# Sliding-window attention beside a gated MLP on one core: query-key products chunk by chunk in two passes, attention sums in pairs, values reloaded in chunks

## The chip, the cores and the metric

One core of a Trainium2 chip. The metric is the time of one execution in device microseconds (us). A kernel is run several times; quoted times are medians of those runs. Runs are marked fast or slow by their granted TensorE clock and time, and only fast runs are compared.

Names of engines: PE is TensorE's matmul, PEld its weight load, DVE is VectorE, ACT is ScalarE, POOL is GpSimd, SP the engine whose queue issues the DMA transfers.

## The reference

Everything is bf16, S = 2048 rows, D = 640, 32 heads of 20, F = 1536.

```python
xn  = layernorm(x)
q, k, v = split(xn @ wqkv)                       # 32 heads of 20
# each row attends to 8 rows: itself and those 2, 4, ... 14 before it
logits = einsum("bhsd,bhswd->bhsw", q, k_gathered) * 20**-0.5    # masked at the start
attn   = softmax(logits)
o      = einsum("bhsw,bhswd->bhsd", attn, v_gathered)
out = x + o @ wo + ((xn @ w_gate) * (xn @ w_up)) @ w_down
```

## The kernel before

The kernel writes its program in one order; a small scheduler gives each instruction to its engine's list in that order and adds semaphore waits where data demand them. So **each engine, and the SP queue, gets its work in exactly the order written**, and an instruction that waits holds those behind it (seen below on DVE at 154.47 us and on SP's queue at 150.47 us).

- Features lie on partitions, rows along the free dimension, in chunks of 128 features (NCH = 5) and pieces of 512 rows (NJ = 4). DVE multiplies Q by K shifted by an offset w (eight offsets, five chunks: 40 products of 128x2048, tile PRD); PE sums within heads with a 0/1 matrix G of 32 columns, four row pieces side by side in the array (tile LOG).
- Values go through memory (v_scratch) and come back as VX, with offsets laid over partitions. DVE multiplies VX by the attention weights ATX (tile P, 20 units of 128x4096: four row pieces j times five chunks c); PE sums each with a 32-column matrix SEL into OT.
- Between these, PE works on a list of "fill": V projections, gate and up products (`glu`), and output rows (`tail`), which add the down projection and OT times WO, 17 matmuls of 320 columns for half the output width. A tail of row piece j may only start once the five units of piece j are done.

```python
    def qk_logits(w, c, s):                       # one product: 4 matmuls of 32 columns
        lb = 6 + w % 2
        for j in range(NJ):
            ... # PS[32j:32j+32, lb] += G[:, c].T @ PRD[:, s, 512 rows of piece j]
        if c == NCH - 1:
            ... # ACT: LOG[slot_of(w)] = PS[lb] * SCALE; POOL: mask

    def vx_load(j):                               # all 20 values of row piece j, 2600 KB
        dst = VX[:, j % 2]
        ...

    def glu(which, m, j):                         # gate or up: 5 matmuls of 512 columns
        ... # ACT: GSX or USX = PS; DVE later: HT = USX * GSX (at most one held back)

    def tail(t, nb):                              # one half of 128 output rows
        b = bank()
        flush_h()
        ... # 12 matmuls with HT, WD and 5 with OT, WO into PS[b]
        op("dve", lambda e: e.tensor_tensor(o, PS[:, b, 0:DHALF], xr, ALU.add), ...)   # FOUT = PS + XR
        if nb == 1:
            stores.append(dma(...))               # the store, and the load of XR for rows t + 3
    ...
    for i in range(10):                           # the last Q and K projections, all of them first
        proj(i % 2, i // 2, 3)
    ...
    add_gu(0)
    add_gu(1)
    fill.append((0.0, lambda: [xr_load(t) for t in range(NXR)]))    # the first three XR loads
    add_dn(0)
    add_gu(2)
    add_dn(1)
    ...
    order = [(w, c) for w in range(W) for c in range(NCH)]          # offset by offset
    for i, (w, c) in enumerate(order):
        ...
        if c in (1, 4):                           # batches of 2 and 3 products
            for a in ready:
                qk_logits(*a)
            ready = []
        run_fill(1.05)
    for st in softmax_steps():                    # whole width, exp in two halves of the offsets
        st()
        run_fill(1.05)
    for j in range(2):
        vx_load(j)
    for j in range(NJ):
        attn_move(j)
    run_fill(12.0)
    units = [(j, c) for j in range(NJ) for c in range(NCH)]
    pv_mul(*units[0])
    for i, (j, c) in enumerate(units):            # one product, one sum
        run_fill(2.1)
        if i + 1 < len(units):
            pv_mul(*units[i + 1])
        if c == NCH - 1 and j + 2 < NJ:
            vx_load(j + 2)
        pv_sum(j, c)
        units_done[0] += 1
```

Of the kernel before, what the change touches and what calls it, by code (L numbers as in the profile page):

```python
# [195 lines left out]
def build_kernel(nc, A_x, A_wqkv, A_wo, B_x, B_w_gate, B_w_up, B_w_down, out):  # L196
# [28 lines left out]
    VX = sb("VX", [128, 2, DH, VW], at=a_qk)  # L225
# [6 lines left out]
    NP = 2  # L232
    P = sb("P", [128, NP, 4, 2, JB], at=a_pr)
    ATX = sb("ATX", [128, 2, S], at=a_pr + NP * 8 * JB * 2)
# [13 lines left out]
    NGX = 3  # L248
    GSX = sb("GSX", [128, NGX, JB])
    USX = sb("USX", [128, NGX, JB])  # L250
# [40 lines left out]
    def wqkv_load(g):  # L291
        dma(WQKV[:, g], wqkv_src[:, :, g * D:(g + 1) * D], w=[WQKV[:, g]], name=f"ld_wqkv{g}")
# [3 lines left out]
    wqkv_load(0)  # L296
# [74 lines left out]
    bank_ctr = [0]  # L371

    def bank():
        bank_ctr[0] += 1
        return (bank_ctr[0] - 1) % 6
# [55 lines left out]
    def qk_logits(w, c, s):  # L431
        lb = 6 + w % 2
        for j in range(NJ):
            o, x = PS[32 * j:32 * j + 32, lb, :], PRD[:, s, j * JB:(j + 1) * JB]
            op("pe", (lambda o, x, j: lambda e: e.matmul(o, G[:, c, :], x, start=(c == 0), stop=(c == NCH - 1),  # L435
                                                      tile_position=(0, 32 * j)))(o, x, j),
               r=[G[:, c, :], x], w=[o], name=f"lg{w}_{c}_{j}")
        if c == NCH - 1:
            o = LOG[:, slot_of(w), :]
            op("act", lambda e: e.activation(o, PS[:, lb, :], ACT.Copy, scale=SCALE), r=[PS[:, lb, :]], w=[o],  # L440
               name=f"lgev{w}")
            if w > 0:
                m = LOG[0:32, slot_of(w), 0:DIL * w]
                op("pool", lambda e: e.memset(m, NEG), w=[m], name=f"mask{w}")

    def softmax_steps():
# [3 lines left out]
        def bc(t, n):  # L450
            return t.unsqueeze(1).to_broadcast([128, n, JB])

        steps = [
            tt(MX[:], LOG[:, 0:4, :], LOG[:, 4:8, :], ALU.max, "smax1"),
            tt(MY[:], MX[:, 0:2, :], MX[:, 2:4, :], ALU.max, "smax2"),
            tt(MZ[:], MY[:, 0, :], MY[:, 1, :], ALU.max, "smax3"),
        ]
        for h in range(2):
            L = LOG[:, 4 * h:4 * h + 4, :]
            steps.append((lambda L: lambda: op("dve", lambda e: e.tensor_tensor(L, L, bc(MZ[:], 4), ALU.subtract),  # L460
                                            r=[L, MZ[:]], w=[L], name="lsub"))(L))
            steps.append((lambda L: lambda: op("act", lambda e: e.activation(L, L, ACT.Exp), r=[L], w=[L],  # L462
                                            name="exp"))(L))

        def recip(e):
            with nc.allow_low_precision("bf16 softmax reciprocal"):
                return e.reciprocal(RS[:], SM[:, 3, :])  # L467

        steps += [
            tt(SM[:], LOG[:, 0:4, :], LOG[:, 4:8, :], ALU.add, "ssum1"),  # L470
            tt(SM[:, 0:2, :], SM[:, 0:2, :], SM[:, 2:4, :], ALU.add, "ssum2"),
            tt(SM[:, 3, :], SM[:, 0, :], SM[:, 1, :], ALU.add, "ssum3"),
            lambda: op("dve", recip, r=[SM[:, 3, :]], w=[RS[:]], name="rs"),
        ]
        steps.append(lambda: op("dve", lambda e: e.tensor_tensor(LOG[:], LOG[:], bc(RS[:], 8), ALU.mult),
                                r=[LOG[:], RS[:]], w=[LOG[:]], name="attn"))
        return steps

# [36 lines left out]
    def flush_h(keep=0):  # L515
        while len(h_pending) > keep:
            h_pending.pop(0)()
# [227 lines left out]
```

## Time and profile before

| | before |
|---|---|
| time, median of the first 3 runs | 293.34 us (292.68 to 293.87) |
| span of the profiled run | 292.2 us |
| PE busy | 279.0 us, 95% |
| start of the 512-column projections | 49.05 us |
| from there to the last output addition | 240.40 us |

The page gives busy time (first line of each engine) and the span in 40 slices, one digit for the busy tenths of each. PEclk is the granted clock in tenths.

```profile
PE 279.0 (95%) x1968; PEld 155.3 (53%) x1986; DVE 172.2 (59%) x252; ACT 118.3 (40%) x211; POOL 2.3 (1%) x17
...
PE   6899999999999999999949999999999999999996
...
PEclk9799999999999999999989999999999999999999
```

PE is the engine to watch: it is busy for 95% of the span, and most of the other work runs beside it. The digit 4 in the middle of its row, near 150 us, is the one big hole. PE's timeline there (start, duration, engine, line, operation, output and inputs, shapes, count, and in brackets the idle time before it and who ended it):

```profile
144.73 1.24 PE L525 MATMUL PS<-XNT,WU 128*128 128x512 bf16 x5
145.91 0.61 PE L505 MATMUL PS<-P,SEL 128*32 128x512 bf16 x8
147.32 0.62 PE L505 MATMUL PS<-P,SEL 128*32 128x512 bf16 x8 [0.80 <-DVE P L496]
149.52 0.61 PE L505 MATMUL PS<-P,SEL 128*32 128x512 bf16 x8 [1.58 <-DVE P L496]
151.72 1.04 PE L505 MATMUL PS<-P,SEL 128*32 128x512 bf16 x8 [1.59 <-DVE P L496]
152.70 2.84 PE L552 MATMUL PS<-WD,HT 128*128 128x320 bf16 x12
155.37 0.84 PE L552 MATMUL PS<-WO,OT 128*128 128x320 bf16 x5
156.14 0.62 PE L505 MATMUL PS<-P,SEL 128*32 128x512 bf16 x8
```

The fill that needs no attention is used up at 145.9 us; PE has only sums to do and waits for each product. Then its clock is low: the same sum takes 1.04 instead of 0.61 us, the next twelve matmuls 2.84 instead of 1.79.

Two small tools are needed. First, *pace*: in undisturbed stretches 50 full-width matmuls of 512 columns take 10.79 us, 0.2158 each, and 272 of 320 columns 36.96 us, 0.1359 each. All matmuls from 49.05 us on (630 of the first kind, 544 of the second, 80 groups of four narrow ones at 0.2158) come to 227.1 us. Second, *the cost of going narrow and back*: a batch of 8 narrow matmuls takes 0.547 us from its start to that of the next group, 0.115 more than two groups at that pace; and a full-width group after it is 0.11 longer (17 output matmuls 2.42 against 2.31 us). That is 0.225 us per batch, and there are 36. So 227.1 + 36 x 0.225 = 235.2, and of the 240.4 us that PE took, 5.2 are loss.

Where DVE was late, and what PE waited for, is in the view of waits (who waited for whom, total us, times, longest):

```profile
DVE PRD L428 <- ACT KT L386: 7.6, 5, 3.9
DVE SM L448 <- ACT LOG L462: 4.1, 1, 4.1
DVE PRD L428 <- PE PS L435: 4.1, 5, 1.1
PE PS L505 <- DVE P L496: 4.0, 3, 1.6
...
PE PS L393 <- DMA WQKV<-in_A_wqkv_dram: 2.0, 1, 2.0
```

### The profile page before, as it was taken

What the parts mean: (1) busy time and instruction counts of PE and PEld (TensorE: products, weight loads), DVE (VectorE), ACT (ScalarE), POOL (GpSimd) and SP (SyncE); (2) the same over time, 40 slices, a digit from 0 to 9 for tenths busy, and PEclk for the clock granted to TensorE, in tenths of its full rate; (3) what the DMA queues carried; (4) which work ended last, traced back from release to release, by engine and by line L of the source; (5) the groups of instructions that cost most, each with busy time, mean ns of one, the idle gap of its engine ahead of it and who ended that gap; (6) DMA issues with size and microseconds to landing.
All of it is one profiled execution on the core that took longest, in us unless ns stands there. A gap on an engine that the chain in (4) does not pass through costs nothing.

```text
span 292.2 us, 4669 instructions
## 1 busy us (share of the span) xinstructions
PE 279.0 (95%) x1968; PEld 155.3 (53%) x1986; DVE 172.2 (59%) x252; ACT 118.3 (40%) x211; POOL 2.3 (1%) x17
## 2 busy tenths in 40 slices
PE   6899999999999999999949999999999999999996
PEld 2789987433333334444315554334577444577774
DVE  4677793588889994497996999961222121222221
ACT  2255555575455455864531124665300455300000
POOL 2000000000000000000000000000000000000000
PEclk9799999999999999999989999999999999999999
DMA  7715999008998008931329385000012100012211
GB/s 227 246 47 76 372 388 273 5 0 342 369 403 325 1 2 273 358 100 36 100 83 342 110 277 179 2 0 0 2 65 69 47 0 0 2 45 90 70 45 45
DMA packets 29556, 39.57 MB, mean 135 GB/s; under 512 B 4192, under 2 KB 25696, under 8 KB 29536
## 3 DMA queue, kind: packets, MB, share of 16 engines
q1 hardware_dynamic: 29536, 39.29, 40.1%
q8 instruction: 15, 0.25, 0.3%
q14 instruction: 5, 0.04, 0.0%
HBM read 25.07 MB, written 13.16 MB: 131 GB/s over the span
## 4 chain that ended last, share of the span: by engine, by line
PE 82%; DVE 8%; ACT 4%; DMA 2%; issue 2%; SPq 0%; DVEq 0%; ACTq 0%
PE PS L525 27%; PE PS L552 26%; PE PS L381 11%; PE PS L400 7%; PE PS L393 4%; DVE P L496 3%; PE PS L435 3%; PE PS L505 3%; DMA XST<-in_A_x_dram 2%; PE PS L357 2%; DVE SM L448 1%; ACT LOG L462 1%; DVE RS L467 1%; ACT USX L527 1%; ACT GSX L527 1%
## 5 line engine op out<-in xcount | busy, mean ns | idle before, releaser
L525 PE MATMUL PS<-XNT,WU 128*128 128x512 bf16 x237 | 59.5, 379 | 0.2
L525 PE MATMUL PS<-XNT,WG 128*128 128x512 bf16 x230 | 57.7, 379 | 1.1 <-issue 0.6
L552 PE MATMUL PS<-WD,HT 128*128 128x320 bf16 x384 | 58.5, 303 | 0.0
L428 DVE TENSOR_TENSOR PRD<-QT,KT 128x2048 bf16<-128x2048 bf16 x40 | 47.0, 1221 | 11.9 <-ACT KT L386 7.6
L527 ACT ACTIVATE GSX<-PS 128x512 bf16<-128x512 f32 x48 | 28.8, 600 | 45.9 <-PE PS L525 32.3
L552 PEld LDWEIGHTS PS<-WD,HT 128*128 128x128 bf16 x384 | 37.3, 99 | 18.7 <-issue 3.8
L496 DVE TENSOR_TENSOR P<-VX,ATX 128x4096 bf16<-128x4096 bf16 x20 | 45.3, 2284 | 0.0
L556 DVE TENSOR_TENSOR FOUT<-PS,XR 128x320 bf16<-128x320 f32 x32 | 15.7, 492 | 46.4 <-PE PS L552 46.4
L532 DVE TENSOR_TENSOR HT<-USX,GSX 128x512 bf16<-128x512 bf16 x48 | 20.1, 423 | 38.7 <-ACT USX L527 38.7
L525 PEld LDWEIGHTS PS<-XNT,WG 128*128 128x128 bf16 x240 | 22.4, 98 | 30.6 <-issue 4.7
L525 PEld LDWEIGHTS PS<-XNT,WU 128*128 128x128 bf16 x240 | 23.1, 98 | 29.1 <-issue 1.7
L527 ACT ACTIVATE USX<-PS 128x512 bf16<-128x512 f32 x48 | 28.8, 601 | 20.5 <-PE PS L525 20.3
L381 PE MATMUL PS<-XNT,WQKV 128*128 128x512 bf16 x145 | 33.3, 380 | 0.4 <-ACT VST L386 0.2
L552 PE MATMUL PS<-WO,OT 128*128 128x320 bf16 x160 | 27.0, 299 | 0.0
L381 PEld LDWEIGHTS PS<-XNT,WQKV 128*128 128x128 bf16 x150 | 14.0, 98 | 19.0 <-issue 2.1
L400 PE MATMUL PS<-XNT,WQKV 128*128 128x256 bf16 x200 | 23.6, 273 | 0.0
L509 ACT ACTIVATE OT<-PS 128x512 bf16<-128x512 f32 x20 | 11.9, 597 | 24.4 <-PE PS L505 24.4
L400 PEld LDWEIGHTS PS<-XNT,WQKV 128*128 128x128 bf16 x200 | 19.1, 98 | 2.0
L552 PEld LDWEIGHTS PS<-WO,OT 128*128 128x128 bf16 x160 | 15.7, 98 | 6.1
L505 PE MATMUL PS<-P,SEL 128*32 128x512 bf16 x160 | 12.7, 396 | 4.0 <-DVE P L496 4.0
L386 ACT ACTIVATE VST<-PS 128x512 bf16<-128x512 f32 x20 | 11.9, 596 | 11.2 <-PE PS L381 11.2
L393 PE MATMUL PS<-XNT,WQKV 128*128 128x128 bf16 x200 | 13.3, 228 | 2.7 <-DMA WQKV<-in_A_wqkv_dram 2.0
(46 smaller groups left out, 142.6 us busy)
## 6 DMA issues: line engine op xcount, KB each, us to landing
VX<-v_scratch SPq DMA_DIRECT2D x4, 2600.0 KB, 11.1
v_scratch<-VST SPq DMA_DIRECT2D x20, 512.0 KB, 5.1
XST<-in_A_x_dram SPq DMA_DIRECT2D x16, 160.0 KB, 3.8
XR<-in_A_x_dram SPq DMA_DIRECT2D x16, 160.0 KB, 2.5
out_dram<-FOUT SPq DMA_DIRECT2D x16, 160.0 KB, 1.8
WQKV<-in_A_wqkv_dram SPq DMA_DIRECT2D x3, 800.0 KB, 6.6
WG<-in_B_w_gate_dram SPq DMA_DIRECT2D x1, 1920.0 KB, 11.6
WU<-in_B_w_up_dram SPq DMA_DIRECT2D x1, 1920.0 KB, 16.0
```

The lines of the kernel that those rows point to most:

```text
L381: op("pe", (lambda l, x, c: lambda e: e.matmul(PS[:, b, :], l, x, start=(c == 0), stop=(c == NCH - 1)))(l, x, c), r=[l, x], w=[PS[:, b, :] ...
L386: op("act", lambda e: e.activation(o, PS[:, b, :], ACT.Copy), r=[PS[:, b, :]], w=[o], name=f"pev{which}_{m}_{j}")
L393: op("pe", (lambda o, l, x, c: lambda e: e.matmul(o, l, x, start=(c == 0), stop=(c == NCH - 1)))(o, l, x, c), r=[l, x], w=[o], name=f"pp{w ...
L400: op("pe", (lambda l, x, c: lambda e: e.matmul(o, l, x, start=(c == 0), stop=(c == NCH - 1)))(l, x, c), r=[l, x], w=[o], name=f"pw{which}_ ...
L428: op("dve", lambda e: e.tensor_tensor(PRD[:, s, :], QT[:, c, :], k, ALU.mult), r=[QT[:, c, :], k], w=[PRD[:, s, :]], name=f"prod{w}_{c}")
L496: op("dve", lambda e: e.tensor_tensor(P[:, u], vw, a, ALU.mult), r=[v, ATX[:, :, j * JB:(j + 1) * JB]], w=[P[:, u]], name=f"pv{j}_{c}")
L505: op("pe", (lambda o, dq, r: lambda e: e.matmul(o, SEL[:], P[:, u, dq, r, :], start=(r == 0), stop=(r == 1), tile_position=(0, 32 * dq)))( ...
L525: op("pe", (lambda l, x, c: lambda e: e.matmul(PS[:, b, :], l, x, start=(c == 0), stop=(c == NCH - 1)))(l, x, c), r=[l, x], w=[PS[:, b, :] ...
L527: op("act", lambda e: e.activation(X[:, k, :], PS[:, b, :], ACT.Copy), r=[PS[:, b, :]], w=[X[:, k, :]], name=f"guev{which}_{m}_{j}")
L532: h_pending.append(lambda: op("dve", lambda e: e.tensor_tensor(o, USX[:, k, :], GSX[:, k, :], ALU.mult), r=[USX[:, k, :], GSX[:, k, :]], w ...
L552: op("pe", (lambda l, x, i: lambda e: e.matmul(PS[:, b, 0:DHALF], l, x, start=(i == 0), stop=(i == n - 1)))(l, x, i), r=[l, x], w=[PS[:, b ...
L556: op("dve", lambda e: e.tensor_tensor(o, PS[:, b, 0:DHALF], xr, ALU.add), r=[PS[:, b, :], xr], w=[o], name=f"fin{t}_{nb}")
```

## The change

The intent: bring DVE's attention work forward so that PE never runs out of fill, with fewer and longer narrow batches.

- Products go chunk by chunk, four offsets at a time, in two passes; they start as soon as the last projection of a chunk is done. Logits are summed in batches of four products (16 matmuls), in four banks.
- Softmax runs in two halves of the rows, so that the exponentials of one overlap DVE's work on the other. Gate multiplies are held back meanwhile (`h_keep`), in place in HT.
- Values are reloaded in 20 pieces of 520 KB, eight ahead; the load for unit u+8 is issued after the product of unit u. Sums are done in pairs, with three product buffers.
- PE's order is now made by a plan: two counters (`t_pe`, `t_dve`) that add up estimated costs.
- At the start the first weight load is split, and the second tile's normalization goes ahead of the third's statistics.

```diff
-    VX = sb("VX", [128, 2, DH, VW], at=a_qk)
+    NVX = 8
+    VX = sb("VX", [128, NVX, 4, VW], at=a_qk)
 ...
-    wqkv_load(0)
+    wqkv_load(0, 0, 2 * 128)
+    wqkv_load(0, 2 * 128, D)
 ...
+    def vx_load(u):
+        j, c = divmod(u, NCH)
+        dst = VX[:, u % NVX]
 ...
+    def pv_mul(u):
 ...
+        op("dve", lambda e: e.tensor_tensor(p[:], vw, a, ALU.mult), r=[v, at], w=[p[:]], name=f"pv{u}")
+        if u + NVX < NU:
+            vx_load(u + NVX)
 ...
+    ln_apply(1)
     ln_stats_a(2)
-    ln_apply(1)
 ...
-    order = [(w, c) for w in range(W) for c in range(NCH)]
+    order = [(w, c) for h in range(2) for c in range(NCH) for w in range(4 * h, 4 * h + 4)]
 ...
+    for u in range(NVX):
+        vx_load(u)
+    bank_ring[:] = bank_ring + [4, 5]
+    h_keep[0] = NUS - 1
+    for cost, st in softmax_steps():
         st()
-        run_fill(1.05)
+        t_dve[0] += cost
+        run_fill(t_dve[0])
+    h_keep[0] = 1
     for j in range(NJ):
         attn_move(j)
 ...
+    t_dve[0] += 3.0
+    for u in range(0, NU, 2):
+        pv_mul(u)
+        if u:
+            run_fill(t_ready)
+            pv_sum((u - 2, u - 1))
+            t_pe[0] = max(t_pe[0], t_ready) + 1.13
+            units_done[0] += 2
+        pv_mul(u + 1)
+        t_dve[0] += 4.57
+        t_ready = t_dve[0] + 0.2
```

The fill list itself is as before.

More of the change, by code (lines that the diff above doesn't have):

```diff
@@ L231, in build_kernel @@
     PRD = sb("PRD", [128, NPW, S])
-    NP = 2
-    P = sb("P", [128, NP, 4, 2, JB], at=a_pr)
-    ATX = sb("ATX", [128, 2, S], at=a_pr + NP * 8 * JB * 2)
+    PB = [sb("PA", [128, 4, 2, JB], at=a_pr), sb("PB", [128, 4, 2, JB], at=a_pr + 8 * JB * 2),
+          sb("PC", [128, 4, 2, JB], at=a_qk + NVX * 4 * VW * 2)]
+    NP = len(PB)
+    ATX = sb("ATX", [128, 2, S], at=a_pr + 2 * 8 * JB * 2)
     MX = sb("MX", [128, 4, JB], at=a_pr)
@@ L247, in build_kernel @@
     FOUT = sb("FOUT", [128, 2, D])
-    NGX = 3
-    GSX = sb("GSX", [128, NGX, JB])
-    USX = sb("USX", [128, NGX, JB])
+    NUS = 6
+    USX = sb("USX", [128, NUS, JB])
     STATS = sb("STATS", [128, 2, 16], FP32)
@@ L289, in build_kernel, with wqkv_load @@
     wqkv_src = A_wqkv.rearrange("(c p) n -> p c n", p=128)
-    def wqkv_load(g):
-        dma(WQKV[:, g], wqkv_src[:, :, g * D:(g + 1) * D], w=[WQKV[:, g]], name=f"ld_wqkv{g}")
+    def wqkv_load(g, lo=0, hi=D):
+        dst = WQKV[:, g, :, lo:hi]
+        dma(dst, wqkv_src[:, :, g * D + lo:g * D + hi], w=[dst], name=f"ld_wqkv{g}_{lo}")
     x_load(0)
     x_load(1)
-    wqkv_load(0)
+    wqkv_load(0, 0, 2 * 128)
+    wqkv_load(0, 2 * 128, D)
     x_load(2)
@@ L368, in warm @@
                r=[ZERO[:]], w=[PS[:, 5, :]], name="warm")
-    bank_ctr = [0]
+    bank_ring = list(range(6))
     def bank():
-        bank_ctr[0] += 1
-        return (bank_ctr[0] - 1) % 6
+        b = bank_ring.pop(0)
+        bank_ring.append(b)
+        return b
     def proj(which, m, j):
@@ L429, in qk_prod, with qk_logits @@
            r=[QT[:, c, :], k], w=[PRD[:, s, :]], name=f"prod{w}_{c}")
-    def qk_logits(w, c, s):
-        lb = 6 + w % 2
-        for j in range(NJ):
-            o, x = PS[32 * j:32 * j + 32, lb, :], PRD[:, s, j * JB:(j + 1) * JB]
-            op("pe", (lambda o, x, j: lambda e: e.matmul(o, G[:, c, :], x, start=(c == 0), stop=(c == NCH - 1),
-                                                      tile_position=(0, 32 * j)))(o, x, j),
-               r=[G[:, c, :], x], w=[o], name=f"lg{w}_{c}_{j}")
-        if c == NCH - 1:
-            o = LOG[:, slot_of(w), :]
-            op("act", lambda e: e.activation(o, PS[:, lb, :], ACT.Copy, scale=SCALE), r=[PS[:, lb, :]], w=[o],
-               name=f"lgev{w}")
-            if w > 0:
-                m = LOG[0:32, slot_of(w), 0:DIL * w]
-                op("pool", lambda e: e.memset(m, NEG), w=[m], name=f"mask{w}")
+    def qk_logits(batch):
+        for w, c, s in batch:
+            lb = 4 + w % 4
+            for j in range(NJ):
+                o, x = PS[32 * j:32 * j + 32, lb, :], PRD[:, s, j * JB:(j + 1) * JB]
+                op("pe", (lambda o, x, j, c: lambda e: e.matmul(o, G[:, c, :], x, start=(c == 0), stop=(c == NCH - 1),
+                                                             tile_position=(0, 32 * j)))(o, x, j, c),
+                   r=[G[:, c, :], x], w=[o], name=f"lg{w}_{c}_{j}")
+        for w, c, s in batch:
+            if c == NCH - 1:
+                lb = 4 + w % 4
+                o = LOG[:, slot_of(w), :]
+                op("act", (lambda o, lb: lambda e: e.activation(o, PS[:, lb, :], ACT.Copy, scale=SCALE))(o, lb),
+                   r=[PS[:, lb, :]], w=[o], name=f"lgev{w}")
+                if w > 0:
+                    m = LOG[0:32, slot_of(w), 0:DIL * w]
+                    op("pool", (lambda m: lambda e: e.memset(m, NEG))(m), w=[m], name=f"mask{w}")
     def softmax_steps():
@@ L448, in tt @@
             return lambda: op("dve", lambda e: e.tensor_tensor(o, a, b, f), r=[a, b], w=[o], name=name)
-        def bc(t, n):
-            return t.unsqueeze(1).to_broadcast([128, n, JB])
-        steps = [
-            tt(MX[:], LOG[:, 0:4, :], LOG[:, 4:8, :], ALU.max, "smax1"),
-            tt(MY[:], MX[:, 0:2, :], MX[:, 2:4, :], ALU.max, "smax2"),
-            tt(MZ[:], MY[:, 0, :], MY[:, 1, :], ALU.max, "smax3"),
-        ]
-        for h in range(2):
-            L = LOG[:, 4 * h:4 * h + 4, :]
-            steps.append((lambda L: lambda: op("dve", lambda e: e.tensor_tensor(L, L, bc(MZ[:], 4), ALU.subtract),
-                                            r=[L, MZ[:]], w=[L], name="lsub"))(L))
-            steps.append((lambda L: lambda: op("act", lambda e: e.activation(L, L, ACT.Exp), r=[L], w=[L],
-                                            name="exp"))(L))
@@ L465, in recip @@
-        def recip(e):
-            with nc.allow_low_precision("bf16 softmax reciprocal"):
-                return e.reciprocal(RS[:], SM[:, 3, :])
-        steps += [
-            tt(SM[:], LOG[:, 0:4, :], LOG[:, 4:8, :], ALU.add, "ssum1"),
-            tt(SM[:, 0:2, :], SM[:, 0:2, :], SM[:, 2:4, :], ALU.add, "ssum2"),
-            tt(SM[:, 3, :], SM[:, 0, :], SM[:, 1, :], ALU.add, "ssum3"),
-            lambda: op("dve", recip, r=[SM[:, 3, :]], w=[RS[:]], name="rs"),
-        ]
-        steps.append(lambda: op("dve", lambda e: e.tensor_tensor(LOG[:], LOG[:], bc(RS[:], 8), ALU.mult),
-                                r=[LOG[:], RS[:]], w=[LOG[:]], name="attn"))
@@ L477, in softmax_steps, with half, bc, recip @@
-        return steps
+        def half(x):
+            cs = slice(x * JB // 2, (x + 1) * JB // 2)
+            def bc(t, n):
+                return t.unsqueeze(1).to_broadcast([128, n, JB // 2])
+            L, M1, M2, M3 = LOG[:, :, cs], MX[:, :, cs], MY[:, :, cs], MZ[:, cs]
+            S1, S2, R = SM[:, 0:4, cs], SM[:, 0:2, cs], RS[:, cs]
+            def recip(e):
+                with nc.allow_low_precision("bf16 softmax reciprocal"):
+                    return e.reciprocal(R, SM[:, 3, cs])
+            head = [
+                (0.67, tt(M1, L[:, 0:4], L[:, 4:8], ALU.max, "smax1")),
+                (0.4, tt(M2, M1[:, 0:2], M1[:, 2:4], ALU.max, "smax2")),
+                (0.25, tt(M3, M2[:, 0], M2[:, 1], ALU.max, "smax3")),
+                (1.22, lambda: op("dve", lambda e: e.tensor_tensor(L, L, bc(M3, 8), ALU.subtract), r=[L, M3], w=[L],
+                                  name="lsub")),
+                (0.0, lambda: op("act", lambda e: e.activation(L, L, ACT.Exp), r=[L], w=[L], name="exp")),
+            ]
+            rest = [
+                (1.2, tt(S1, L[:, 0:4], L[:, 4:8], ALU.add, "ssum1")),
+                (0.67, tt(S2, S1[:, 0:2], S1[:, 2:4], ALU.add, "ssum2")),
+                (0.4, tt(SM[:, 3, cs], S2[:, 0], S2[:, 1], ALU.add, "ssum3")),
+                (1.75, lambda: op("dve", recip, r=[SM[:, 3, cs]], w=[R], name="rs")),
+                (1.22, lambda: op("dve", lambda e: e.tensor_tensor(L, L, bc(R, 8), ALU.mult), r=[L, R], w=[L],
+                                  name="attn")),
+            ]
+            return head, rest
@@ L479, in attn_move @@
+        (h0, r0), (h1, r1) = half(0), half(1)
+        return h0 + h1 + r0 + r1
     def attn_move(j):
@@ L483, in attn_move @@
             dma(dst, src, r=[src], w=[dst], name=f"atx{j}_{wq}")
-    def vx_load(j):
-        dst = VX[:, j % 2]
-        src = vscr.rearrange("q (h d) s -> (q h) d s", d=DH)[:, :, j * JB:j * JB + VW]
-        dma(dst, src, r=[("vscr", m, q) for m in range(NCH + 1) for q in range(4)], w=[dst], name=f"vx{j}")
-    def pv_mul(j, c):
-        u = (j * NCH + c) % NP
-        v = VX[:, j % 2, 4 * c:4 * c + 4, :]
-        vw = bass.AP(v.tensor, v.offset, [v.ap[0], [VW, 4], [8, 2], [1, JB]])
-        a = ATX[:, :, j * JB:(j + 1) * JB].unsqueeze(1).to_broadcast([128, 4, 2, JB])
-        op("dve", lambda e: e.tensor_tensor(P[:, u], vw, a, ALU.mult),
-           r=[v, ATX[:, :, j * JB:(j + 1) * JB]], w=[P[:, u]], name=f"pv{j}_{c}")
@@ L499, in pv_sum @@
-    def pv_sum(j, c):
-        u = (j * NCH + c) % NP
-        b = 6 + (j * NCH + c) % 2
-        for r in range(2):
-            for dq in range(4):
-                o = PS[32 * dq:32 * dq + 32, b, :]
-                op("pe", (lambda o, dq, r: lambda e: e.matmul(o, SEL[:], P[:, u, dq, r, :], start=(r == 0), stop=(r == 1),
-                                                           tile_position=(0, 32 * dq)))(o, dq, r),
-                   r=[SEL[:], P[:, u, dq, r, :]], w=[o], name=f"I{j}_{c}_{dq}_{r}")
-        o = OT[:, c, j * JB:(j + 1) * JB]
-        op("act", lambda e: e.activation(o, PS[:, b, :], ACT.Copy), r=[PS[:, b, :]], w=[o], name=f"oev{j}_{c}")
+    def vx_load(u):
+        j, c = divmod(u, NCH)
+        dst = VX[:, u % NVX]
+        src = vscr.rearrange("q (h d) s -> (q h) d s", d=DH)[:, 4 * c:4 * c + 4, j * JB:j * JB + VW]
+        dma(dst, src, r=[("vscr", m, q) for m in range(NCH + 1) for q in range(4)], w=[dst], name=f"vx{u}")
@@ new lines, in pv_mul, with pv_sum @@
+    def pv_mul(u):
+        j = u // NCH
+        v, p = VX[:, u % NVX], PB[u % NP]
+        vw = bass.AP(v.tensor, v.offset, [v.ap[0], [VW, 4], [8, 2], [1, JB]])
+        at = ATX[:, :, j * JB:(j + 1) * JB]
+        a = at.unsqueeze(1).to_broadcast([128, 4, 2, JB])
+        op("dve", lambda e: e.tensor_tensor(p[:], vw, a, ALU.mult), r=[v, at], w=[p[:]], name=f"pv{u}")
+        if u + NVX < NU:
+            vx_load(u + NVX)
+    def pv_sum(us):
+        for u in us:
+            b, p = 6 + u % 2, PB[u % NP]
+            for r in range(2):
+                for dq in range(4):
+                    o = PS[32 * dq:32 * dq + 32, b, :]
+                    op("pe", (lambda o, p, dq, r: lambda e: e.matmul(o, SEL[:], p[:, dq, r, :], start=(r == 0), stop=(r == 1),
+                                                                  tile_position=(0, 32 * dq)))(o, p, dq, r),
+                       r=[SEL[:], p[:, dq, r, :]], w=[o], name=f"I{u}_{dq}_{r}")
+        for u in us:
+            j, c = divmod(u, NCH)
+            b = 6 + u % 2
+            o = OT[:, c, j * JB:(j + 1) * JB]
+            op("act", (lambda o, b: lambda e: e.activation(o, PS[:, b, :], ACT.Copy))(o, b), r=[PS[:, b, :]], w=[o],
+               name=f"oev{u}")
@@ L512, in build_kernel, with flush_h @@
     pair_ctr = [0]
     h_pending = []
-    def flush_h(keep=0):
+    h_keep = [1]
+    def flush_h(keep):
+        n = 0
         while len(h_pending) > keep:
             h_pending.pop(0)()
+            n += 1
+        return n
     def glu(which, m, j):
-        k = pair_ctr[0] % NGX
-        T, X = ((WG, GSX), (WU, USX))[which]
+        k = pair_ctr[0] % NUS
+        T = (WG, WU)[which]
+        h = HT[:, j % 2, m, :]
+        o = (h, USX[:, k, :])[which]
         b = bank()
@@ L526, in glu @@
                r=[l, x], w=[PS[:, b, :]], name=f"gu{which}_{m}_{j}_{c}")
-        op("act", lambda e: e.activation(X[:, k, :], PS[:, b, :], ACT.Copy), r=[PS[:, b, :]], w=[X[:, k, :]],
-           name=f"guev{which}_{m}_{j}")
+        op("act", lambda e: e.activation(o, PS[:, b, :], ACT.Copy), r=[PS[:, b, :]], w=[o], name=f"guev{which}_{m}_{j}")
         if which == 1:
             pair_ctr[0] += 1
-            o = HT[:, j % 2, m, :]
-            h_pending.append(lambda: op("dve", lambda e: e.tensor_tensor(o, USX[:, k, :], GSX[:, k, :], ALU.mult),
-                                        r=[USX[:, k, :], GSX[:, k, :]], w=[o], name=f"h{m}_{j}"))
-            flush_h(1)
+            h_pending.append(lambda: op("dve", lambda e: e.tensor_tensor(h, h, o, ALU.mult), r=[h, o], w=[h],
+                                        name=f"h{m}_{j}"))
+            return 0.43 * flush_h(h_keep[0])
+        return 0.0
     def xr_load(t):
@@ L544, in tail @@
         b = bank()
-        flush_h()
+        flush_h(0)
         n = NF + NCH
@@ L623, in build_kernel @@
                 tr()
+    NU = NJ * NCH
+    t_pe, t_dve = [40.0], [41.0]
+    last_qk = []
     for i in range(10):
-        proj(i % 2, i // 2, 3)
-        if i % 2 == 1:
-            tr()
+        last_qk.append((i // 2, (lambda i: lambda: (proj(i % 2, i // 2, 3), tr() if i % 2 == 1 else None))(i)))
     for q in range(4):
@@ L660, in build_kernel, with run_fill @@
     pos = [0]
-    def run_fill(us):
-        while us > 0 and pos[0] < len(fill):
+    def run_fill(until):
+        while t_pe[0] < until and pos[0] < len(fill):
             it = fill[pos[0]]
@@ L667, in run_fill @@
                     return
-                us -= 2.31
+                t_pe[0] += 2.31
                 it[2]()
             else:
-                us -= it[0]
-                it[1]()
+                t_pe[0] += it[0]
+                d = it[1]()
+                t_dve[0] += d if isinstance(d, float) else 0.0
             pos[0] += 1
-    order = [(w, c) for w in range(W) for c in range(NCH)]
-    LA = 3
-    for i in range(LA):
-        qk_prod(*order[i], i % NPW)
-    ready = []
-    for i, (w, c) in enumerate(order):
-        if i + LA < len(order):
-            qk_prod(*order[i + LA], (i + LA) % NPW)
-        ready.append((w, c, i % NPW))
-        if c in (1, 4):
-            for a in ready:
-                qk_logits(*a)
-            ready = []
-        run_fill(1.05)
@@ L689, in build_kernel @@
-    for st in softmax_steps():
-        st()
-        run_fill(1.05)
-    for j in range(2):
-        vx_load(j)
+    order = [(w, c) for h in range(2) for c in range(NCH) for w in range(4 * h, 4 * h + 4)]
+    bank_ring[:] = [b for b in bank_ring if b < 4]
+    batch, ready = [], None
+    for i, (w, c) in enumerate(order):
+        while c < NCH and w < 4 and last_qk and last_qk[0][0] <= c:
+            last_qk.pop(0)[1]()
+            t_pe[0] += 1.08
+        t_dve[0] = max(t_dve[0], t_pe[0] + 0.8 if w == 0 and i < 20 else 0.0) + 1.22
+        qk_prod(w, c, i % NPW)
+        batch.append((w, c, i % NPW))
+        if ready is not None and len(batch) == 2:
+            while last_qk and t_pe[0] < ready[1]:
+                last_qk.pop(0)[1]()
+                t_pe[0] += 1.08
+            run_fill(ready[1])
+            qk_logits(ready[0])
+            t_pe[0] = max(t_pe[0], ready[1]) + 1.13
+            ready = None
+        if len(batch) == 4:
+            ready = (batch, t_dve[0] + 0.2)
+            batch = []
@@ L694, in build_kernel @@
+    run_fill(ready[1])
+    qk_logits(ready[0])
+    t_pe[0] = max(t_pe[0], ready[1]) + 1.13
+    t_dve[0] = max(t_dve[0], t_pe[0] + 2.5)
+    for u in range(NVX):
[3 more added lines that the diff above has]
+    for cost, st in softmax_steps():
+        st()
+        t_dve[0] += cost
+        run_fill(t_dve[0])
+    h_keep[0] = 1
     for j in range(NJ):
         attn_move(j)
-    run_fill(12.0)
-    units = [(j, c) for j in range(NJ) for c in range(NCH)]
@@ L698, in build_kernel @@
-    pv_mul(*units[0])
-    for i, (j, c) in enumerate(units):
-        run_fill(2.1)
-        if i + 1 < len(units):
-            pv_mul(*units[i + 1])
-        if c == NCH - 1 and j + 2 < NJ:
-            vx_load(j + 2)
-        pv_sum(j, c)
-        units_done[0] += 1
+    t_dve[0] += 3.0
[9 more added lines that the diff above has]
+        t_ready = t_dve[0] + 0.2
@@ L707, in build_kernel @@
+    run_fill(t_ready)
+    pv_sum((NU - 2, NU - 1))
+    units_done[0] += 2
     while pos[0] < len(fill):
-        run_fill(1.0)
+        run_fill(1e9)
     K.emit(stores)
```

## The prediction

> **What bounds the kernel now.** TensorE (PE): busy 279.0 of 292.2 us (page, first part); DVE 59%, ScalarE 40%; the chain of waits is 82% PE. Only PE time that is waste can be won. Timelines by engine show four kinds:
>
> 1. *Idle and cold clock, 145 to 155 us.* The fill work (V projections, gate/up products of stages 0 and 1) runs out at 145.9. Three attention sums wait 0.80, 1.58 and 1.59 us for DVE's P products, since the next fill (output rows) needs five units. Then the clock reads 0.83: a sum takes 1.04 instead of 0.61 us, twelve output matmuls 2.84 instead of 1.79. Loss: 4.0 + 1.4 = 5.4 us.
> 2. *Switching between full-width and 32-column matmuls.* A batch of 8 of the latter takes 0.55 us, of 12 0.76: 0.215 per four plus 0.115 fixed. The full-width group after it is longer too: 17 output matmuls 2.42 us against 2.31 in the last stretch. About 0.225 us per batch, times 36 (16 logits, 20 sums) = 8.1 us. The Trainium skill, "TensorEngine Tiling (Array Packing)", Key Properties, says that changing the tiling mode drains the engine; this trace agrees, 0.11 us each way.
> 3. *Start.* The first projection waits for the weight load until 8.40 us (PE idle 2.0); the second tile's normalization sits on DVE behind statistics of a tile that lands at 8.78. The long projection block starts only at 10.4.
> 4. DVE is late (cause of 1): QK products wait 0.93 us per K chunk from 51.8 to 60.4, later 1.15 us at a time for PE; softmax runs from 114.8 to 135.1, 4.1 of it waiting for exponentials; the first P product starts at 139.9.
>
> **What the change does.** 10 logit and 10 sum batches of 16: 20 instead of 36, 16 x 0.225 = 3.6 us less, all on PE. Products go four offsets per chunk, so DVE runs from about 52 us nearly without waiting (40 x 1.2), ends near 103; softmax in halves hides the exponentials (ends near 123); first P product near 128. Fill then lasts until six units are done (near 144, some five fill units left), and the 5.4 us go. Split weight load and earlier normalization: about 1.5 us. The in-place gate multiply removes ScalarE's 13.6 us of waiting for DVE (view of waits), off the path: worth nothing. VX traffic is unchanged, in pieces of 520 KB; eight should land before softmax ends.
>
> **What it gives back.** PE's fixed order plans 4.57 us of DVE per pair of units. Two products take 4.4, but the output-row additions (0.41 each, not in the plan) make 5.0 at 1.5 rows per pair. So in the first output stage (some 5 pairs) PE waits about 0.4 us per pair, and about 1 at the first pair, as the moves took 4.8 us before and the plan allows 3. Estimate: 3 us of new waits.
>
> **Sum.** 293.3 - 5.4 - 3.6 - 1.5 + 3 = 285.8; the new waits may be smaller, so I put 285.0, range 281.5 to 288.5. Faster by over 2% 0.80, within 2% 0.18, slower 0.02.
>
> **The profile, if right:** 20 batches at about 0.98 us; no long PE gap before the sums; first P product at 126 to 130; clock 1.00 after 20 us; PE's waits for P in pieces under 1 us; first projection near 6.5. **If wrong:** one long gap before the first sum; waits on VX loads; PE waiting for evictions with only four banks for fill; batches of 16 longer than 1 us.
>
> **What would make it wrong.** VX pieces late, or the moves queued behind them; DVE waiting for product buffers held by PE's fixed order; the split load landing no earlier, its rows being shorter; a gap that lowers the clock again.

## The result, and the profile after

| | before | after |
|---|---|---|
| time, median of 4 runs each | 293.61 us | 289.16 us (288.98 to 289.46) |
| ratio, 95% interval | | 0.9851 (0.982 to 0.9882) |
| span of the profiled run | 292.2 us | 287.3 us |
| start of the 512-column projections | 49.05 us | 47.53 us |
| from there to the last output addition | 240.40 us | 236.99 us |
| narrow batches (groups of one tile side by side counted once) | 36 | 20 |

Ratios are the mean time of one kernel's fast runs over that of the other's of the same rounds, so they are not quite the ratio of the medians.

The kernel is 1.5% faster; 285.0 had been expected, with a range of 281.5 to 288.5. With a line drawn at 2% the result is "same", to which the prediction had given 0.18.

```profile
PE 275.4 (96%) x1968; PEld 156.7 (55%) x1986; DVE 171.4 (60%) x260; ACT 116.1 (40%) x211; POOL 2.3 (1%) x17
...
PE   7899999999999999998997999999999999999996
...
PEclk9999999999999999999999799999999999999999
```

The hole in PE's row near 150 us is gone; there are two shallower ones, at 130 and at 155 to 160 us. The ledger says how much they hold: 227.1 + 20 x 0.225 = 231.6 us of needed PE time against 236.99, so 5.4 us are loss, **as much as before**. PE's timeline at the two places:

```profile
130.44 1.25 PE L550 MATMUL PS<-XNT,WG 128*128 128x512 bf16 x5
132.90 1.25 PE L550 MATMUL PS<-XNT,WU 128*128 128x512 bf16 x5 [1.20 <-ACT USX L552]
...
155.05 0.62 PE L520 MATMUL PS<-PC,SEL 128*32 128x512 bf16 x8
157.61 0.61 PE L520 MATMUL PS<-PA,SEL 128*32 128x512 bf16 x8 [1.95 <-DVE PA L510]
158.16 3.37 PE L576 MATMUL PS<-WD,HT 128*128 128x320 bf16 x12
```

The waits that answer to those shown of before:

```profile
ACT USX L552 <- DVE HT L555: 8.0, 2, 7.5
...
DVE PRD L432 <- ACT KT L390: 4.2, 1, 4.2
...
DVE FOUT L580 <- DMA XR<-in_A_x_dram: 3.8, 1, 3.8
...
PE PS L520 <- DVE PA L510: 1.9, 1, 1.9
...
PE PS L550 <- ACT USX L552: 1.2, 1, 1.2
```

PE's wait for WQKV is gone, DVE's wait for exponentials (SM) is down to 0.8 us, and its products (PRD) wait for PE only twice in the timeline, 0.23 and 0.55 us. But there is a wait that the kernel before did not have: an output addition of DVE (FOUT) waits 3.8 us for XR, a plain load of input rows. DVE's timeline there, and SP's, where each line is a run of DMA issues (start, time on the queue):

```profile
147.76 2.28 DVE L510 TENSOR_TENSOR PC<-VX,ATX 128x4096 bf16<-128x4096 bf16 x1
149.96 0.75 DVE L555 TENSOR_TENSOR HT<-HT,USX 128x512 bf16<-128x512 bf16 x2
154.47 0.89 DVE L580 TENSOR_TENSOR FOUT<-PS,XR 128x320 bf16<-128x320 f32 x2 [3.76 <-DMA XR<-in_A_x_dram]
155.28 2.28 DVE L510 TENSOR_TENSOR PA<-VX,ATX 128x4096 bf16<-128x4096 bf16 x1
157.48 2.28 DVE L510 TENSOR_TENSOR PB<-VX,ATX 128x4096 bf16<-128x4096 bf16 x1
```

```profile
121.12 12.11 SPq L269 DMA_DIRECT2D ATX<-LOG  x16
133.27 17.16 SPq L269 DMA_DIRECT2D VX<-v_scratch  x9
150.47 1.46 SPq L269 DMA_DIRECT2D XR<-in_A_x_dram  x3
```

The kernel before issued its first XR loads right after the moves of the attention weights (ATX), with no load between them that waited for a product:

```profile
135.10 10.68 SPq L268 DMA_DIRECT2D ATX<-LOG  x16
145.84 1.56 SPq L268 DMA_DIRECT2D XR<-in_A_x_dram  x3
```

Read together, for the changed kernel: the VX load of unit 16 stands in SP's list ahead of the XR loads, and must wait until the product of unit 8 has been computed (147.76 + 2.2 = 149.96). Only then, at 150.47, is XR issued; it lands at 154.4. DVE has nothing else it may do, as the addition comes first in its order. From 154.47 on DVE works without a gap, 3.8 us late, and PE waits for it at 155.7.

The other wait: five gate multiplies held back during softmax were put in DVE's order only with the first fill after it, behind the third P product (it ends at 131.7 us). Until then ACT could not reuse USX (7.5 us), the banks of PE filled up, and PE stood for 1.2 us.

### The profile page after: what moved, and what is told of

Same layout as the page of the kernel before. It is cut to its first block, busy times and chain, and to the rows that moved or that the text cites. A ratio compares the mean times of both kernels' runs of the same rounds, so it can differ in the third digit from the quotient of the medians.

```text
span 287.3 us, 4706 instructions
## 1 busy us (share of the span) xinstructions
PE 275.4 (96%) x1968; PEld 156.7 (55%) x1986; DVE 171.4 (60%) x260; ACT 116.1 (40%) x211; POOL 2.3 (1%) x17
## 4 chain that ended last, share of the span: by engine, by line
PE 72%; DVE 15%; DMA 4%; issue 4%; ACT 2%; SPq 2%; DVEq 0%; ACTq 0%
PE PS L550 27%; PE PS L576 19%; PE PS L385 11%; PE PS L404 7%; PE PS L440 3%; DVE PC L510 3%; DVE PB L510 3%; DMA XST<-in_A_x_dram 2%; PE PS L397 2%; DVE PA L510 2%; SPq L269 2%; DVE SM L455 2%; DMA XR<-in_A_x_dram 1%; PE PS L360 1%; DVE RS L468 1%
## 5 line engine op out<-in xcount | busy, mean ns | idle before, releaser
L432 DVE TENSOR_TENSOR PRD<-QT,KT 128x2048 bf16<-128x2048 bf16 x40 | 45.8, 1220 | 5.0 <-ACT KT L390 4.2
L552 ACT ACTIVATE HT<-PS 128x512 bf16<-128x512 f32 x48 | 29.1, 605 | 39.6 <-PE PS L550 39.6
L555 DVE TENSOR_TENSOR HT<-HT,USX 128x512 bf16<-128x512 bf16 x48 | 19.1, 420 | 39.5 <-ACT USX L552 39.5
L527 ACT ACTIVATE OT<-PS 128x512 bf16<-128x512 f32 x20 | 11.1, 600 | 22.3 <-PE PS L520 22.1
L510 DVE TENSOR_TENSOR PA<-VX,ATX 128x4096 bf16<-128x4096 bf16 x7 | 16.0, 2285 | 4.0 <-DMA ATX<-LOG 4.0
L510 DVE TENSOR_TENSOR PB<-VX,ATX 128x4096 bf16<-128x4096 bf16 x7 | 16.0, 2285 | 0.2 <-PE PS L520 0.2
L510 DVE TENSOR_TENSOR PC<-VX,ATX 128x4096 bf16<-128x4096 bf16 x6 | 13.7, 2285 | 0.2 <-PE PS L520 0.2
```

The costliest lines, as they stand in the source:

```text
L432: op("dve", lambda e: e.tensor_tensor(PRD[:, s, :], QT[:, c, :], k, ALU.mult), r=[QT[:, c, :], k], w=[PRD[:, s, :]], name=f"prod{w}_{c}")
L510: op("dve", lambda e: e.tensor_tensor(p[:], vw, a, ALU.mult), r=[v, at], w=[p[:]], name=f"pv{u}")
L527: op("act", (lambda o, b: lambda e: e.activation(o, PS[:, b, :], ACT.Copy))(o, b), r=[PS[:, b, :]], w=[o], name=f"oev{u}")
L552: op("act", lambda e: e.activation(o, PS[:, b, :], ACT.Copy), r=[PS[:, b, :]], w=[o], name=f"guev{which}_{m}_{j}")
L555: h_pending.append(lambda: op("dve", lambda e: e.tensor_tensor(h, h, o, ALU.mult), r=[h, o], w=[h], name=f"h{m}_{j}"))
```

## The experiments

Two theories were set against each other. **Theory 1**: the new loss is two matters of order, XR behind a waiting VX load in SP's queue (about 3 us), and held-back multiplies (about 1.2 us). **Rival 2**: it is the loss that I had predicted; DVE needs 5.0 us per pair of units in the output stage where the plan allows 4.57, so the XR wait only takes the place of waits for P. All runs have 5 rounds, with the kernel before on the same chip. The calls: r_after, e1, e2, e3 (before: 292.64 us median), e4 to e7 (292.94), e8, e9, e4_again (292.91; only three fast runs of before, hence the wide intervals). The first call ran on one chip and the other two on another, where the changed kernel itself was not run again: where e4 to e9 are set against it or against e3, the kernel before, 0.3 us apart in the medians of the calls, is the link.

| run | time, us | ratio to before (95%) | starts 512-column work, us | from there to last addition, us |
|---|---|---|---|---|
| r_after (as changed) | 289.26 | 0.9872 (0.9839 to 0.9905) | 47.53 (first profile) | 236.99 |
| e1 XR early | 286.09 | 0.9764 (0.9735 to 0.9793) | 47.39 | 234.30 |
| e2 multiplies before first product | 288.05 | 0.9832 (0.98 to 0.9865) | 47.21 | 235.87 |
| e3 both | 284.83 | 0.9721 (0.969 to 0.9753) | 47.55 | 232.97 |
| e4 both, and additions in the plan | 283.28 | 0.9673 (0.9645 to 0.97) | 47.03 | 231.52 |
| e4_again | 283.79 | 0.9647 (0.9583 to 0.9711) | 47.76 | 231.52 |
| e9 as e4, old start | 284.70 | 0.9688 (0.96 to 0.9776) | 47.88 | 231.52 |
| e8 XR from ACT's queue | 285.90 | 0.9724 (0.9648 to 0.9799) | 47.10 | 234.04 |
| e6 logit batches cut in two | 290.46 | 0.9911 (0.9884 to 0.9938) | 47.60 | 238.45 |
| e5 before, new start only | 292.72 | 0.9991 (0.9962 to 1.002) | 47.23 | 241.08 |
| e7 before, fill not used up | 287.16 | 0.9797 (0.9767 to 0.9826) | 47.45 | 235.15 |

### r_after: the changed kernel again

> The changed kernel again, as the yardstick of this call. Both theories: ratio to before 0.985 (within 0.003), 288.7 to 289.6 us. Its profile should again show one XR wait of DVE near 3.8 us and one wait of PE for HT/USX near 1.2 us; if these are missing in a second look they are not the cause.

289.26 us, ratio 0.9872. The run that was profiled was slow (granted clock 0.95, 296.31 us) and isn't read for durations; it shows the XR wait again, 3.8 us, but only 0.2 us of PE's USX wait. The fast profiles of e1, e6 and e8, which keep the order of the multiplies, show that second wait again: 7.5 us of ACT, 1.2 us of PE.

### e1_xr_early: the first three XR loads ahead of the products

```diff
-    fill.append((0.0, lambda: [xr_load(t) for t in range(NXR)]))
 ...
+    for t in range(NXR):
+        xr_load(t)
     batch, ready = [], None
```

> Edit: the first three XR loads are issued before the query-key products, so they no longer stand in the SP queue behind a VX load that waits for a P product. Theory 1 (XR late in the queue; DVE waits 3.8 us, PE follows): DVE's XR wait gone, PE's 1.95 us wait and the slow clock after it gone, time 2.5 to 3.5 us shorter than the changed kernel (285.6 to 286.7). Rival 2 (the stage is paced by DVE's products and additions, about 5.0 us per pair against 4.57 planned, as I had predicted): the XR wait goes but PE waits for P in small pieces instead, gain under 1 us (288.2 or more). A mixture (gain 1 to 2.5) would mean that both hold.

286.09 us, 3.2 us below r_after. DVE's XR wait is gone, PE's 1.95 us wait with it, and the clock is 1.00. What is left of waits for P is one of 0.87 us. Theory 1 holds; rival 2 holds for under a microsecond.

### e2_h_flush: held-back multiplies into DVE's idle time

```diff
     h_keep[0] = 1
+    t_dve[0] += 0.34 * flush_h(1)
     for j in range(NJ):
         attn_move(j)
```

> Edit: the gate multiplies held back during softmax are put before the first P product (DVE is idle 4 us there, waiting for ATX) instead of behind the third. Theory 1: ScalarE's 7.5 us wait for HT and PE's 1.2 us wait for USX go, time about 1.2 us shorter than the changed kernel (287.8 to 288.2). Rival: PE is waiting for DVE a little later anyway, so the time stays within 0.4 us.

288.05 us, 1.2 us below r_after. ACT's 7.5 us wait and PE's wait for USX are gone; DVE's idle time before the first product fell from 4.0 to 2.7 us. The XR wait (3.7 us) and PE's wait for it (1.9) are still there. The edit also adds the cost of the multiplies to the plan's DVE counter, so that PE's order shifts a little (first sum at 131.52 us instead of 129.46); the two were not tried apart.

### e3_both

> Both edits. Theory 1: the gains add, 3.7 to 4.7 us below the changed kernel (284.4 to 285.5, ratio to before about 0.970), PE's idle time between 47 us and the end below 1 us. Rival 2: under 1.5 us below it, with PE waits for P of about 0.4 us per pair of units in the first output stage.

284.83 us, 4.4 us below r_after: 3.2 + 1.2, so the two waits are separate. DVE and PE where XR was missing before, and PE's only wait for P:

```profile
148.81 0.76 DVE L555 TENSOR_TENSOR HT<-HT,USX 128x512 bf16<-128x512 bf16 x2
149.48 0.48 DVE L580 TENSOR_TENSOR FOUT<-PS,XR 128x320 bf16<-128x320 f32 x1
150.62 0.49 DVE L580 TENSOR_TENSOR FOUT<-PS,XR 128x320 bf16<-128x320 f32 x1 [0.65 <-PE PS L576]
151.18 2.29 DVE L510 TENSOR_TENSOR PA<-VX,ATX 128x4096 bf16<-128x4096 bf16 x1
```

```profile
172.04 0.61 PE L520 MATMUL PS<-PB,SEL 128*32 128x512 bf16 x8
173.54 0.62 PE L520 MATMUL PS<-PC,SEL 128*32 128x512 bf16 x8 [0.88 <-DVE PC L510]
```

The second addition now waits for PE's matmuls, as it should, and not for its input. The rate that I had predicted is real: between the products that start at 151.18 and 161.19 us DVE goes through two pairs of units with three additions, 5.0 us per pair. But PE was not waiting at the door. When the stage began, the product of unit 7 had been ready 3.9 us before PE came to its pair (146.6 to 150.5). This lead was used up by the fourth pair (unit 13, at 163.5 us), and the wait shown, at the sixth pair, is the only one above 0.1 us.

### e4_plan: the additions counted in the plan

```diff
                 t_pe[0] += 2.31
+                t_dve[0] += 0.41
                 it[2]()
```

> Edit: on top of e3 the plan of PE's order counts 0.41 us of DVE for each output-row addition. My predicted term (0.4 us of wait per pair, 3 us in all) showed in e3's trace as one wait of 0.88 us only. If that wait comes from the uncounted additions, it goes, and the time falls by 0.5 to 0.9 us against e3 (to a ratio of about 0.969 to before). If not (order not the cause), ratio as e3, 0.972.

283.28 us; by the ratios 0.5% below e3, about 1.4 us. That is more than the 0.5 to 0.9 expected. In the trace the stretch after 47 us is 1.45 us shorter: the gap between the two halves of one sum batch (1.50 us from start to start instead of 0.44) is the main part. No wait for P is left on PE's list:

```profile
PE PS L370 <- DVE EPSC L273: 1.3, 1, 1.3
PE PS L397 <- ACT KT L412: 0.7, 1, 0.7
PE PS L360 <- DVE XNS L349: 0.6, 3, 0.3
PE PS L550 <- issue: 0.3, 2, 0.2
PE PS L385 <- issue: 0.3, 2, 0.2
```

The first three are before 47 us; the rest are places where the trace lacks a matmul record. And the ledger closes: 231.52 us against 231.6 of needed PE time.

### e4_again and e8_xr_act: the order of issue, or the traffic?

e1 moved the XR loads both out of SP's waiting line and out of the VX traffic. e8 leaves them at their place in the program, but has ACT's queue issue them:

```diff
-        dma(XR[:, t % NXR, :], xhbm[...], w=[...], name=f"xr{t}")
+        dma(XR[:, t % NXR, :], xhbm[...], w=[...], name=f"xr{t}", eng="act" if t < NXR else "sp")
```

> The changed kernel, the first three XR loads at the same place of the program but issued from ScalarE's queue, so that they do not stand behind a VX load that waits for a P product; the same DMA traffic runs beside them. Theory (the order of issue in SP's queue makes XR late): they are issued near 147 us instead of 150.5, DVE's wait for XR falls from 3.8 to under 1.5 us, and the time falls 1.5 to 3.2 us below the changed kernel (286.0 to 287.7). Rival (the data path is full of VX, so XR lands late whoever issues it): landing takes 5 us or more, the wait stays above 2.5 us, gain under 1 us.

> e4 once more, as the yardstick of this call: ratio to before 0.967 within 0.002, no PE wait above 0.3 us after 47 us.

e8: 285.90 us, 3.3 us below the changed kernel (289.2), as much as e1 and 0.1 more than the range given. XR is issued from 146.71 us on, beside the same VX transfers; its landing takes 3.4 us (median of three, the longest 5.4), no less than in the changed kernel (at most 3.9), and no addition waits for it:

```profile
146.71 2.49 ACTq L269 DMA_DIRECT2D XR<-in_A_x_dram  x3
```

So the order of issue was the cause, not the traffic. The Trainium skill, "DMA: Bandwidth & Descriptors", Issuing engines are not separate DMA queues, says that all transfers end up on the same 16 DMA engines and that issuing from several engines only saves the time to initiate them. The landing times do not contradict the first half; the second half leaves out what mattered here, that an issue waiting for a semaphore holds those behind it (3.3 us of the kernel's time).

e4_again: 283.79 us, and the same 231.52 us after the start; its ratio of 0.9647 lies just below the 0.965 to 0.969 expected, but has an interval of 0.0064 either way; the difference of 0.5 us from the first e4 is in the start (47.76 against 47.03).

### e5_start_only and e9_old_start: what is the start worth?

e5 is the kernel before with the two start edits of the change alone (split weight load, normalization first).

> The kernel before with only the start's part of the change: the first weight load in two pieces and the second tile's normalization ahead of the third's statistics. If the start is worth what the traces show (the 512-column projections begin at 47.53 instead of 49.05 us): 1.3 to 1.7 us shorter than before, ratio 0.994 to 0.9955. If the later waits swallow it: ratio above 0.998.

292.72 us, ratio 0.9991; the interval excludes the 1.5 us that I had put. In its trace the first attention sum comes 1.81 us earlier than before, at 141.28, but the last addition only 1.14: in the hole near 147 us the low clock lasted longer (twelve output matmuls 3.38 us instead of 2.84).

e9 is e4 with the start edits taken back.

> e4 with the start of before put back (one weight load, the third tile's statistics first). The start part alone gave 0.2 us on the kernel before, with an interval of 0.6% either way, where its trace gave 1.8 us at 47 us and lost 0.7 of it again in the gap near 147 us. Theory (worth 1.5 us where nothing later waits): 1.3 to 1.9 us slower than e4, ratio to before 0.9715 to 0.974. Rival (the start is worth nothing): within 0.4 us of e4, ratio 0.967 to 0.9685.

284.70 us against 283.79: by the ratios 0.4%, 1.2 us, just under what was expected, but with a spread: its six runs lie between 283.59 and 286.82, those of e4_again between 283.47 and 283.89. Its profiled run starts the 512-column work at 47.88, hardly later than with the new start. So does e7 (47.45), which has the old start too. The 49.05 us of the profile before was one late case of a start that varies; with the new start all nine fast profiles lie between 47.03 and 47.76.

The two traces show where it was lost. Of its 1.17 us against e9, 0.40 is a later arrival of the first weights (PE's wait for them ends at 8.40 instead of 8.00 us); the rest is PE work at a low clock after that wait of 2.02 us (0.81 and 0.85 in the 5 us stretches from 5 and 10 us, against 1.00 in e9 and e7, where PE waited 0.97 and 1.20 us). The three longest runs of e9 are also the ones with a granted clock below 1.000 (0.987 and twice 0.994; all of e4_again have 0.999 or more), so such a dip may be what spreads them; they were not profiled. By the runs, the edit is worth between nothing and some 3 us, about 1 us in the mean.

### e6_split_logits: what does a narrow batch cost?

Nine of the ten logit batches are cut in two, with one full-width unit between; the work is the same.

```diff
-            qk_logits(ready[0])
-            t_pe[0] = max(t_pe[0], ready[1]) + 1.13
+            qk_logits(ready[0][:2])
+            t_pe[0] = max(t_pe[0], ready[1]) + 0.66
+            if last_qk:
+                last_qk.pop(0)[1]()
+                t_pe[0] += 1.08
+            else:
+                run_fill(t_pe[0] + 0.1)
+            qk_logits(ready[0][2:])
+            t_pe[0] += 0.66
```

> The changed kernel with each logit batch of 16 cut into two of 8 with a full-width unit between: 20 logit batches instead of 10, the same work. Theory (each change of tile width costs PE 0.11 us, 0.22 us per batch there and back): 2.2 us longer than the changed kernel's 289.2 (ratio to before about 0.995). Rival (the switch is hidden, or only a trace artefact of modelled matmul ends): same time as the changed kernel, ratio 0.987. Part of it may be hidden behind later waits of PE for DVE; then between 1.2 and 2.2 us.

(The last batch stayed whole, so nine more batches and not ten: 2.0 us by the theory.) 290.46 us, about 1.3 us above the changed kernel. In the trace the first output tail starts later, by 1.97 us after the start is taken off:

```profile
148.99 1.79 PE L576 MATMUL PS<-WD,HT 128*128 128x320 bf16 x12
150.62 0.84 PE L576 MATMUL PS<-WO,OT 128*128 128x320 bf16 x5
```

(changed kernel: 146.95 us; start 47.60 against 47.53). That is 0.22 us per batch, as read from the profile before. The rest is hidden, as the wait for XR comes anyway. The Trainium skill, "TensorEngine Tiling (Array Packing)", Key Properties, says that a change of tiling mode drains the engine; the runs agree that the change costs time, and give the price; whether it is a drain, or something else that comes with narrow matmuls, they do not separate.

### e7_no_exhaustion: was the hole in the kernel before a lack of fill?

The kernel before, with a wrong result: tails of the first row piece read XNT instead of OT, so they need no sums, and may start three units earlier.

```diff
-                if units_done[0] < NCH * (it[1] + 1):
+                if units_done[0] < NCH * (it[1] + 1) - (3 if it[1] == 0 else 0):
 ...
-                l, x = OT[:, i - NF, t * TS:(t + 1) * TS], WO[:, i - NF, cols]
+                l, x = (XNT if j == 0 else OT)[:, i - NF, t * TS:(t + 1) * TS], WO[:, i - NF, cols]
```

> The kernel before, with a result that is wrong on purpose: the first four output tiles read XNT in place of OT, so they need no attention sums and may start after the second unit; PE's work stays the same size. Theory (fill runs out, PE idles 4.0 us and then runs 1.4 us long at the slow clock): 4 to 5.4 us shorter than before, ratio 0.982 to 0.987, no PE gap above 1 us near 147 us and no clock dip. Rival (PE is waiting for DVE's products whatever the fill): less than 1.5 us gained, the waits for P moved later.

287.16 us, ratio 0.9797, 5.9 us by the ratio; a little above the range given. PE goes on without a gap and the clock stays at 1.000:

```profile
144.31 0.61 PE L505 MATMUL PS<-P,SEL 128*32 128x512 bf16 x8
144.86 1.80 PE L552 MATMUL PS<-WD,HT 128*128 128x320 bf16 x12
146.50 0.84 PE L552 MATMUL PS<-WO,XNT 128*128 128x320 bf16 x5
147.27 0.61 PE L505 MATMUL PS<-P,SEL 128*32 128x512 bf16 x8
```

After the start it needs 235.15 us; 235.2 had been worked out for a kernel of 36 batches without loss.

## Why the prediction was wrong

Point by point, with what the runs put in each place:

- *"the 5.4 us go"*: right. The hole is gone; e7 shows that it was worth 5.3 us of PE time (240.40 - 235.15).
- *"16 x 0.225 = 3.6 us less"*: right. Each batch costs 0.22 us in e6, and e4 and e7 land on the sums worked out with 0.225.
- *"Split weight load and earlier normalization: about 1.5 us"*: too large. One profile had been read as if it were typical. The start varies; e5 and e9 give 0.3 and 1.2 us.
- *"Estimate: 3 us of new waits"*: **this is the step that failed.** New loss was 5.5 us (236.99 - 231.52, the changed kernel against e4), and of other kinds than the prediction had it:
  - *"PE waits about 0.4 us per pair, and about 1 at the first pair"*: the rate of 5.0 us per pair was right, but PE entered the stage with a lead of DVE of 3.9 us over it, so only 0.88 us of wait showed in e3; at the first pair there was no wait. With the additions in the plan (e4) the stretch got 1.45 us shorter in all, so the kind of wait that the prediction named was worth at most half of the 3 us put down for it.
  - Not foreseen: XR behind a VX load in SP's queue, 3.2 us (e1, and e8 for the reason; 2.7 us of it in e1's trace after the start). The prediction had named late VX pieces and late moves among what could go wrong; VX was in time, and a load that the diff does not touch was late.
  - Not foreseen: held-back multiplies behind the third product, 1.2 us (e2; 1.1 in its trace). The prediction had said of ACT's waits that they are off the path and worth nothing. The old ones were; the new one, 7.5 us, was long enough to fill PE's banks.
- DVE was early, as predicted or more so: first P product at 125.1 us (128 predicted, 139.9 before).

The sum with measured terms: 5.3 + 3.6 + about 1 - 5.5 = 4.4 us; measured 293.61 - 289.16 = 4.45. The sum on record came to 7.5 (and the 285.0 put down to 8.3). That three of the terms fit is no test, since 5.3, 3.6 and 5.5 come out of the same stretches; what is tested apart from them is the 3.6: e7 and e4, both without loss, differ by 3.63 us (235.15 - 231.52), for 16 x 0.225 = 3.60 predicted.

So the gain did not shrink at the place it was meant for. PE's loss was taken out at 147 us, and as much came back elsewhere (that the sizes agree is chance): 4.0 us as two waits of the new order (e3's trace), the rest as waits that the plan had not counted (e4). With both mended and the plan corrected (e4) the same change is worth 9.7 us by the medians (ratio 0.9673), against 0.9872 for the changed kernel, so 2.0% faster still, and the result is correct.

What stays open: how the low clock after the waits comes about. The profiled run of the changed kernel had it after a gap of 1.95 us (twelve matmuls 3.37 us instead of 1.79), the other three of its four runs had a clock of 1.000 and spans of 287.6, 287.7 and 287.3 us, no shorter than the 287.3 of the profiled one. So it seems to have cost nothing there, as DVE set the pace; when it comes is not shown.

## What to carry to other kernels

When loads become finer and are issued "after the product that frees the buffer", every later issue on the same queue inherits that wait: go through the queue in program order and ask of each small load what stands ahead of it, also of loads that the change does not touch. A deferral (here the held-back multiplies) needs a place where it is paid back, in the idle time and not behind the next long instruction. And before pricing a change, work out what the limiting engine must do at its own pace and what each profile loses against it: here the loss before (5.2 us), after (5.4) and in e4 (none) tells at once that the change had moved its waits and not removed them.

## What the Trainium skill lacked or had wrong

- "TensorEngine Tiling (Array Packing)", Key Properties: says that a change of tiling mode drains the engine, but gives no price. Here 0.11 us each way, 0.22 to 0.225 us per narrow batch (e6: 1.97 us for nine).
- "DMA: Bandwidth & Descriptors", Issuing engines are not separate DMA queues: says that issuing from another engine only saves the time to initiate. It lacks the waiting line: an issue that waits for a semaphore holds those behind it. (The page does say, of the anatomy of one DMA, that the wait happens on the issuing sequencer; it does not say what that costs later issues.) Three loads of 160 KB moved from SP's to ACT's queue at the same place of the program took 3.3 us off the kernel, though they landed no sooner after their issue (median 3.4, longest 5.4 us, against at most 3.9).
- "TensorE: Matmul & The Clock Gate", Why this matters for your kernels: advises against PE-idle gaps of more than about 3 us. Here single gaps of 1.6 us or less, three of them with sums of 0.6 us between (kernel before), and one of 1.95 us (one run of the changed kernel) were followed by matmuls at about half rate; other runs of the changed kernel kept a clock of 1.000. (Of short idling the page says, in A second HAM failure mode, that it can lower the clock when it is frequent, but gives no length; a single wait of 1.62 us in e6 left the clock at 1.000.)
